# Batch 1's transposes by DMA, keys of batch 2 loaded sooner, and the first x in halves: an attention and FFN kernel on one core

## The chip, the cores and the metric

The kernel runs on one core of a Trainium2 chip. The metric is the device time of one execution in microseconds (us). Seven runs of the kernel before the change took 249.07 to 250.13 us, with a median of 249.35 us.

## The reference

Two stages follow each other. An attention without softmax (a "cosformer") is computed for 8 batches of 8 heads, 576 positions and head dimension 64; its output, as 4608 tokens of 512 values, goes through an FFN in which two projections are multiplied with each other.

```python
# q, k, v: [8, 8, 576, 64]; theta = pi/2 * pos / 576
def phi(x, c, s):
    r = np.maximum(x, 0.0)
    return np.concatenate([r * c, r * s], axis=-1)      # 64 -> 128 features
q_p, k_p = phi(q, cos_w, sin_w), phi(k, cos_w, sin_w)
kv = np.einsum('bhsf,bhsd->bhfd', k_p, v)
z = np.sum(k_p, axis=2)
num = np.einsum('bhsf,bhfd->bhsd', q_p, kv)
den = np.einsum('bhsf,bhf->bhs', q_p, z)[..., None] + 1e-06
x = (num / den).transpose(0, 2, 1, 3).reshape(4608, 512)
# FFN: w1, w2 [512, 1024], w3 [1024, 1024], w_out [1024, 512]
out = ((x @ w1) * (x @ w2)) @ w3 @ w_out
```

## The kernel before

**Attention.** Each batch is cut into five chunks: four of 128 positions and one (chunk 4) of 64. Even batches take them in the order 0, 1, 2, 3, 4, odd batches in the order 4, 0, 1, 2, 3. The inputs are loaded by the POOL queue (`load`, lines 133 and 137, each tensor in a part 0 of 320 KB and a part 1 of 256 KB for the inner batches). `features` (lines 265 to 272) makes the cosine half of the features on DVE and the sine half on ACT. `kv_chunk` multiplies keys with values and sums up over the chunks in the PSUM tile `pnum`; column 64 of each head's values is one, so z comes along. The sum is copied to `kvs`.

The queries must stand with their features on the partitions. There are two ways to that. `q_tr` transposes a chunk's 8 heads on TensorE (PE) and copies the result from PSUM to `qpT`. In the other, `prep_q` issues one DMA transpose from the SP queue (line 283). `dma_q(b)` lists the chunks of a batch that go the second way: none of batch 0, chunks 1, 2 and 3 of batch 1, and all from batch 2 on.

`num(b, c)` multiplies `qpT` with `kvs` for the 8 heads (line 355) into `pnum`, of which there is one buffer, and `normalize` divides on DVE (lines 363 to 365: add, reciprocal, multiply), giving `xblk`, 512 values per token. Chunk 0 of batch 0 has a PSUM tile of its own, `pfirst`.

`x_tr(b, c)` transposes `xblk` into `xT`, which holds 512 tokens per FFN tile. In batches 0 and 1 it uses four PE transposes (line 392) and a copy from PSUM on ACT or DVE (line 394); from batch 2 on it is one DMA transpose on the SP queue (line 387). The tokens of batch 1 fill the rest of FFN tile 1 and the start of tile 2.

**FFN.** There are nine tiles (t) of 512 tokens. For each, `ffn_groups` gives matmuls with w1b and w2b (line 464), a copy `asb` on ACT and the product `abT` on DVE, and then matmuls with w34b (line 510). w34b is w3 times w_out, made in the kernel while tile 0 is worked on (`w3_tr`, line 220, and `w34_mm`, line 232). Tile 0 starts in quarters of 128 tokens, so that PE has work as soon as the first x is there.

**Order.** The schedule is manual: each engine's instructions run in the order in which the program writes them. `ffn_groups` is a generator; after each of its steps the work listed in `slots[g]` is written. For tile 0 the list is made by hand. In slot 15 stands a second list, `between`, spread over the 16 steps of `w34_mm`, whose entries 16 to 23 go to the later slots and 24 to 31 to tile 1. `attention_at(1, between, kv, tr, nu, xt)` places batch 1's steps by the position in the order 4, 0, 1, 2, 3: `tr` where a chunk is transposed on PE, `nu` where `num` stands, and `xt` where `x_tr` stands. From batch 2 on `plan_batch` does this with a fixed pattern.

Loads on the POOL queue are held back by tiny copies: `behind_k`, `behind_q` and `behind_x` copy one element of a result to `seen` (line 540), so that POOL waits for it, and then issue the load. `other_loads` is such a sequence, released by the first `xblk`: the remaining weights, w3 in eight parts, and k, q and v of batch 1. The DMA transposes of SP and the loads of POOL use the same 16 DMA engines.

Of the kernel before, what the change touches and what calls it, by code (L numbers as in the profile page):

```python
# [13 lines left out]
ALU = mybir.AluOpType  # L14
# [3 lines left out]
H, S, D = 8, 576, 64  # L18
# [50 lines left out]
def kernel(  # L69
# [11 lines left out]
    nc = tc.nc  # L81
# [28 lines left out]
    def load_first(eng, t, src, c0=0, n=4, b=0, rows=slice(0, P)):  # L110
        at = src[b, :, 0:512, :].rearrange("h (p j) d -> p h j d", j=4)
        eng.dma_start(out=t[rows, :, c0:c0 + n, :].rearrange("p h j d -> p h (j d)"),  # L112
                      in_=at[rows, :, c0:c0 + n, :].rearrange("p h j d -> p h (j d)"))

    def load_first4(eng, t, src, b=0):
        eng.dma_start(out=t[0:64, :, 4, :], in_=src[b, :, 512:S, :].rearrange("h p d -> p h d"))

    def raw_tile(name):
        return ld.tile([P, H, NCH, D], BF16, name=name + "s", bufs=2 if name == "k" else 1)

    def load(b, which, part=None):
        for name in which:
            src = {"k": k, "v": v, "q": q}[name]
            if part != 1:
                raw[b, name] = raw_tile(name)
            if b in own:
                half = slice(64 * part, 64 * part + 64)
                load_first(nc.gpsimd, raw[b, name], src, b=b, rows=half)
                if part == 1:
                    load_first4(nc.gpsimd, raw[b, name], src, b=b)  # L130
                continue
            if part != 1:
                nc.gpsimd.dma_start(
                    out=raw[b, name][0:64, :, :, :].rearrange("p h j d -> p h (j d)"),
                    in_=src[b, :, 0:320, :].rearrange("h (p j) d -> p h (j d)", j=5))
            if part != 0:
                nc.gpsimd.dma_start(
                    out=raw[b, name][64:128, :, 0:4, :].rearrange("p h j d -> p h (j d)"),
                    in_=src[b, :, 320:S, :].rearrange("h (p j) d -> p h (j d)", j=4))
# [9 lines left out]
    def load_w3(jp):  # L149
        nc.gpsimd.dma_start(out=w3b[:, jp, :], in_=moe_w3[ts(jp, P), :])  # L150
# [36 lines left out]
    identb = const.tile([P, P], BF16, name="identb")  # L187
# [4 lines left out]
    def load_w12(c0, n):  # L192
        nc.gpsimd.dma_start(out=w1b[:, :, ds(c0, n)], in_=w1v[:, :, ds(c0, n)])
        nc.gpsimd.dma_start(out=w2b[:, :, ds(c0, n)], in_=w2v[:, :, ds(c0, n)])
# [6 lines left out]
    def other_loads(behind):  # L201

        seen = sm.tile([P, 1], BF16, name="seen", bufs=1)
        nc.gpsimd.tensor_copy(out=seen[:], in_=behind)
        nc.gpsimd.dma_start(out=w2b[:, :, ds(512, 256)], in_=w2v[:, :, ds(512, 256)])
        load_w12(768, 256)
        nc.gpsimd.dma_start(out=woutb[:], in_=moe_w_out.rearrange("(c p) m -> p c m", p=P))
        for jp in range(8):
            load_w3(jp)
            if jp == 4:  # L210
                load(1, "k")
        load(1, "qv")


    w3Ts = {}
# [22 lines left out]
    def order_of(b):  # L238

        return [0, 1, 2, 3, 4] if b % 2 == 0 else [4, 0, 1, 2, 3]  # L240

    def dma_q(b):

        return order_of(b)[5 if b == 0 else 2 if b == 1 else 0:]

    feat = {}

# [5 lines left out]
    att = {}  # L253
# [91 lines left out]
    def num(b, c, chain=True):  # L345
        rows = out_rows(b, c)
        R = ROWS[c]
        at = columns_of(b, c) - rows.start
        qpT, kvs = att[b]["qpT"], att[b]["kvs"]
        if b == 0 and c == 0:  # L350
            nt = ps_first.tile([P, 2, 512], FP32, name="pfirst")
        else:
            nt = ps_att.tile([P, 2, 512], FP32, name="pnum")
        for h in range(H):
            nc.tensor.matmul(nt[:, h // 4, ds((h % 4) * 65, 65)], lhsT=qpT[:, h, ds(at, 128)],  # L355
                             rhs=kvs[:, h, :], start=True, stop=True)
        n4 = nt[rows, :, 0:260].rearrange("p g (h e) -> p g h e", e=65)
        xblk = sm.tile([P, 2, 4, D], BF16, name="xblk", bufs=6)
        att[b]["x"][c] = xblk

        def normalize():
            den = sm.tile([P, 2, 4], FP32, name="den")
            nc.vector.tensor_scalar_add(out=den[rows], in0=n4[:, :, :, 64], scalar1=1e-6)  # L363
            nc.vector.reciprocal(out=den[rows], in_=den[rows])
            nc.vector.tensor_tensor(out=xblk[rows], in0=n4[:, :, :, 0:D],  # L365
                                    in1=den[rows].unsqueeze(3).to_broadcast([R, 2, 4, D]),
                                    op=ALU.mult)

        if chain:
            normalize()  # L370
        return normalize

    xT = {}

    def x_tr(b, c, by_vector=False, pst=None):
        R, rows = ROWS[c], out_rows(b, c)
        xblk = att[b]["x"].pop(c)
        xf = xblk[rows].rearrange("p g h d -> p (g h d)")
        if b % 2 == 0:
            slot = S * b + 128 * c  # L380
        else:
            slot = S * b + (0 if c == 4 else 64 + 128 * c)
        t, o = divmod(slot, 512)
        if t not in xT:
            xT[t] = xtp.tile([P, 4, 512], BF16, name="xT")
        if b >= 2:
            nc.sync.dma_start_transpose(out=xT[t][:, :, ds(o, R)], in_=xf)
            return
        if pst is None:
            pst = ps_tr.tile([P, 8, 128], BF16, name="pst")  # L390
        for kc in range(4):
            nc.tensor.transpose(pst[:, kc, 0:R], xf[:, ts(kc, 128)], identb[rows, rows])  # L392
        copy = nc.vector.tensor_copy if by_vector else nc.scalar.copy
        copy(out=xT[t][:, :, ds(o, R)], in_=pst[:, 0:4, 0:R])  # L394

    def attention_at(b, slots, kv, tr, nu, xt):

# [151 lines left out]
    def behind_q(b, i, *what):  # L549
        behind(feat[b][1][0:64, order_of(b)[i], 0, 0:1], *what)  # L550
# [37 lines left out]
    for c in range(NCH):  # L588
# [19 lines left out]
         pst=unread[:, :].bitcast(BF16).rearrange("p (a b) -> p a b", b=128))  # L608
# [13 lines left out]
    for t in range(NT):  # L622
        slots = [[] for _ in range(24)]
        if t == 0:
            slots[1].append(lambda: x_tr(0, 1, by_vector=True))
            slots[1].append(lambda: q_tr(0, 3, evac=False)[1]())
            slots[1].append(lambda: num(0, 2))
            slots[3].append(lambda: num(0, 3))
            slots[3].append(lambda: x_tr(0, 2))
            slots[5].append(lambda: x_tr(0, 3))  # L630
            slots[6].append(lambda: prep_q(0, 4))
            slots[11].append(lambda: feature_buffers(1))
            slots[8].append(lambda: q_tr(0, 4))
            slots[10].append(lambda: num(0, 4))
            slots[12].append(lambda: x_tr(0, 4))
            slots[14].append(lambda: w3_tr(0))
            between = [[] for _ in range(32)]
            spread(prep_units(1, (prep_k,)), 6, 8, between)
            spread(prep_units(1, (prep_q,)), 10, 12, between)
            spread(prep_units(1, (prep_v,)), 13, 13, between)  # L640
            attention_at(1, between, kv=(14, 14, 14, 14, 14), tr=(12, 13, 17, 18, 19),
                         nu=(15, 17, 19, 20, 25), xt=(20, 20, 21, 22, 27))
            later = between[24:32]
            for i in range(2):
                between[11 + i].append(lambda i=i: behind_q(1, 2 + 2 * i, 2, "k", i))
            for i, g in enumerate((15, 17, 17, 19)):
                between[g].append(lambda i=i: behind_x(1, (i + 1) // 2, 2, "vvqq"[i], i % 2))
            for jp in range(8):
                for part in range(2):
                    if part == 0 and jp < 7:  # L650
                        slots[15].append(lambda jp=jp: w3_tr(jp + 1))
                    slots[15].append(lambda jp=jp, part=part: w34_mm(jp, part))
                    slots[15] += between[2 * jp + part]
            for g in range(16, 24):
                slots[g] += between[g]
            slots[16].append(open_held)
        elif t == 1:
            for g, units in enumerate(later):
                slots[g] += units
        for g in range(24):  # L660
            slots[g] += plan[24 * t + g]
        for g, _ in enumerate(ffn_groups(t)):
            for u in slots[g]:
                u()
# [30 lines left out]
```

## Time and profile before

| | before |
|---|---|
| median of 7 runs | 249.35 us |
| the profiled execution | 249.5 us |
| its span from first to last instruction | 247.7 us |
| PE busy | 241.5 us |
| VectorE (DVE) busy | 142.7 us |
| ScalarE (ACT) busy | 123.1 us |
| GpSimd (POOL) busy | 94.0 us |
| granted TensorE clock | full |
| HBM traffic over the span | 195 GB/s |

The profile comes from one execution; its own time is 0.15 us above the median of the runs. Times in it count from the first instruction. "The chain of waits" is the work that ended last, followed back step by step to what released it. PE is TensorE's matmul stream and PEld its loading of weights, which overlaps with it; a matmul's end is modelled, so neighbouring matmuls overlap in the timeline, and what PE needs for one is read from the distance between starts or from the chain. A bracket behind an instruction of the timeline tells how long its engine stood idle before it, and on whose result. For a DMA the time to landing runs from its issue to its semaphore.

### The profile page before, as it was taken

The numbers are of one execution on the slowest core, as the hardware profiler recorded it, in microseconds if no ns is written. First come the engines' busy times: TensorE is split into PE (matmuls) and PEld (weight loads), VectorE is DVE, ScalarE is ACT, GpSimd is POOL, SyncE is SP. The second block draws the span as 40 slices with busy tenths as digits, with TensorE's granted clock in tenths as the row PEclk, the third lists the DMA queues.
The fourth block names the chain that finished last, engine by engine and source line by source line (L and its number), as shares of the span: only waits on it lengthen the run. The fifth ranks groups of instructions, "written<-read, shape, count | busy, mean of one in ns | idle before, by whom it ended". The sixth has DMA issues, their size and how long they took to land.

```text
span 247.7 us, 4927 instructions
## 1 busy us (share of the span) xinstructions
PE 241.5 (98%) x1839; PEld 127.4 (51%) x1839; DVE 142.7 (58%) x333; ACT 123.1 (50%) x209; POOL 94.0 (38%) x189
## 2 busy tenths in 40 slices
PE   8899999999999999999999999999999999999994
PEld 2478555565454545544544555455545554444443
DVE  7776674756658555748465866576586555312421
ACT  2576324927762594268426832773287332323331
POOL 7655142215512442154113621562153007875400
PEclk9999999999999999999999999999999999999999
DMA  6999999999999999999999899999985927998713
GB/s 192 177 194 198 210 204 205 145 154 190 167 128 203 148 138 137 150 153 168 138 128 151 110 157 150 154 179 137 149 112 148 210 57 170 285 294 271 211 40 131
DMA packets 86087, 41.15 MB, mean 166 GB/s; under 512 B 53552, under 2 KB 82608, under 8 KB 86064
## 3 DMA queue, kind: packets, MB, share of 16 engines
q0 software_dynamic: 37072, 27.20, 74.0%
q1 hardware_dynamic: 48560, 13.18, 33.1%
q10 hardware_dynamic: 432, 0.46, 0.5%
q8 instruction: 14, 0.23, 0.3%
q14 instruction: 9, 0.07, 0.1%
HBM read 38.80 MB, written 9.44 MB: 195 GB/s over the span
## 4 chain that ended last, share of the span: by engine, by line
PE 93%; DMA 3%; DVE 1%; issue 1%; POOL 1%; ACT 0%; POOLq 0%
PE ffnps L464 50%; PE ffnps L510 24%; PE ffnps L232 6%; PE pnum L355 4%; PE pnum L297 4%; DMA qs<-in_q_dram 3%; PE pst L220 1%; PE pst L392 1%; PE pst L328 1%; PE ffnps L527 1%; POOL vs L112 0%; DVE xblk L365 0%; PE pfirst L355 0%; ACT xT L394 0%; DVE qpT L342 0%
## 5 line engine op out<-in xcount | busy, mean ns | idle before, releaser
L505 DVE TENSOR_TENSOR abT<-asb,ffnps 128x512 bf16<-128x512 bf16 x68 | 46.6, 686 | 55.1 <-PE ffnps L464 54.3
L464 PE MATMUL ffnps<-xT,w1b 128*128 128x512 bf16 (+2 forms) x320 | 74.9, 357 | 0.4 <-ACT xT L394 0.2
L464 PE MATMUL ffnps<-xT,w2b 128*128 128x512 bf16 (+2 forms) x320 | 74.9, 357 | 0.0
L510 PE MATMUL ffnps<-w34b,abT 128*128 128x512 bf16 x280 | 65.8, 379 | 0.0
L501 ACT CAST asb<-ffnps 128x512 bf16<-128x512 f32 x68 | 39.8, 585 | 48.6 <-PE ffnps L464 47.2
L516 ACT COPY held<-ffnps 128x512 f32<-128x512 f32 x35 | 20.5, 586 | 49.6 <-PE ffnps L510 47.6
L464 PEld LDWEIGHTS <-w1b 128*128 128x128 bf16 x320 | 28.9, 98 | 27.7 <-issue 0.6
L464 PEld LDWEIGHTS <-w2b 128*128 128x128 bf16 x320 | 28.7, 98 | 26.9
L510 PEld LDWEIGHTS <-abT 128*128 128x128 bf16 x280 | 25.6, 98 | 26.4
L269 ACT ACTIVATE qp<-qs,sinv 128x512 bf16<-128x512 bf16 (+2 forms) x40 | 28.3, 716 | 3.2 <-DMA qs<-in_q_dram 3.2
L365 DVE TENSOR_TENSOR xblk<-pnum,den 128x512 bf16<-128x512 f32 (+1 forms) x39 | 27.0, 691 | 2.2
L438 POOL DMA_DIRECT2D out_dram<-held x42 | 22.2, 534 | 6.4 <-DMA out_dram<-held 3.7
L269 ACT ACTIVATE kp<-ks,sinv 128x512 bf16<-128x512 bf16 (+1 forms) x35 | 24.5, 721 | 0.0
L540 POOL COPY seen<-xblk 64x1 bf16<-64x1 bf16 x15 | 2.8, 184 | 53.3 <-DVE xblk L365 53.3
L355 PEld LDWEIGHTS <-qpT 128*128 128x128 bf16 x320 | 15.0, 98 | 10.2 <-issue 2.7
L265 DVE TENSOR_SCALAR qp<-qs,cosv 128x512 bf16<-128x512 bf16 (+1 forms) x40 | 17.4, 439 | 2.0 <-DMA qs<-in_q_dram 2.0
L540 POOL COPY seen<-qp 64x1 bf16<-64x1 bf16 x14 | 2.6, 184 | 40.4 <-DVE qp L265 40.4
L363 DVE TENSOR_SCALAR den<-pnum 128x8 f32<-128x8 f32 (+1 forms) x39 | 6.4, 165 | 19.4 <-PE pnum L355 19.4
L289 POOL COPY va<-vs 128x512 bf16<-128x512 bf16 (+1 forms) x30 | 17.5, 632 | 0.0
L297 PEld LDWEIGHTS <-kp 128*128 128x128 bf16 x280 | 13.0, 98 | 7.3
L355 PE MATMUL pnum<-kvs,qpT 128*128 128x65 bf16 x312 | 16.4, 194 | 0.0
L232 PE MATMUL ffnps<-woutb,w3T 128*128 128x512 bf16 x64 | 15.4, 379 | 0.0
(87 smaller groups left out, 184.5 us busy)
## 6 DMA issues: line engine op xcount, KB each, us to landing
out_dram<-held POOLq DMA_DIRECT2D x16, 256.0 KB, 5.1
out_dram<-held POOLq DMA_DIRECT2D x24, 128.0 KB, 4.1
qs<-in_q_dram POOLq DMA_DIRECT2D x10, 256.0 KB, 5.9
w3b<-in_moe_w_dram POOLq DMA_DIRECT2D x8, 256.0 KB, 13.1
ks<-in_k_dram POOLq DMA_DIRECT2D x8, 256.0 KB, 6.5
vs<-in_v_dram POOLq DMA_DIRECT2D x8, 256.0 KB, 6.7
ks<-in_k_dram POOLq DMA_DIRECT2D x6, 320.0 KB, 6.0
qs<-in_q_dram POOLq DMA_DIRECT2D x6, 320.0 KB, 5.7
```

The source lines that it names most:

```text
L232: nc.tensor.matmul(acc[:, :], lhsT=w3T[:, lc, :], rhs=woutb[:, lc, :], start=(lc == 0), stop=(lc == 7))
L269: nc.scalar.activation(out=dst[:R, c, 0:n, D:F], in_=src[:R, 0:n, c, :], func=ACTF.Relu, scale=sinv[:R, at:at + 1], bias=0.0)
L289: eng.tensor_copy(out=feat_of(b)[2][:R, c, :, 0:D], in_=raw[b, "v"][:R, :, c, :])
L297: nc.tensor.matmul(kvt[:, h // 4, ds((h % 4) * 65, 65)], lhsT=kp[:, c, h, :], rhs=va[:, c, h, 0:D + 1], start=(i == 0 and h % 4 == 0), sto ...
L355: nc.tensor.matmul(nt[:, h // 4, ds((h % 4) * 65, 65)], lhsT=qpT[:, h, ds(at, 128)], rhs=kvs[:, h, :], start=True, stop=True)
L365: nc.vector.tensor_tensor(out=xblk[rows], in0=n4[:, :, :, 0:D], in1=den[rows].unsqueeze(3).to_broadcast([R, 2, 4, D]), op=ALU.mult)
L438: eng.dma_start(out=rows[:, :, cols], in_=osb[64 * i:64 * i + rows.shape[0], :, cols])
L464: nc.tensor.matmul(out, lhsT=w[:, kc, ts(jc, 128)], rhs=x[:, kc, tok], start=(kc == 0), stop=(kc == 3))
L501: nc.scalar.copy(out=asb[:], in_=aT[:, :])
L505: nc.vector.tensor_mul(out=abT[:, jc, :], in0=asb[:], in1=bT[:, :])
L510: nc.tensor.matmul(ops[:, :], lhsT=abT[:, jc, ts(ms, 128)], rhs=w34b[:, jc, :], start=(jc == 0), stop=(jc == 7))
L516: nc.scalar.copy(out=osb[:, ms % 2, :], in_=ops[:, :])
```

## The change

It has four parts.

- Batch 1: chunk 0 of the queries joins chunks 1 to 3 on the DMA path (`dma_q`). `x_tr` of chunks 3 and 4 becomes a DMA transpose on SP. Their places in the order (`xt`) go from 20 to 15 for chunk 4 and from 27 to 25 for chunk 3, right behind their `num`. `x_tr` keeps the reference to `xblk`, because `behind_x` reads it afterwards.
- Keys of batch 2: part 0 is loaded at the end of `other_loads` instead of behind the query features of chunk 1 of batch 1, part 1 behind those of chunk 4 instead of chunk 3. (The position in the order, not the chunk number, is what `behind_q` takes: before, positions 2 and 4; after, position 0.)
- The first x (batch 0, chunk 0): the multiply of `normalize` runs in two halves of four heads, and `x_tr` transposes two blocks and copies them, then the other two, both on DVE.
- Chunk 3 of batch 0: `x_tr` likewise runs in two halves; the first is copied by ACT, the second by DVE.

```diff
@@ other_loads
         load(1, "qv")
+        load(2, "k", 0)
@@ dma_q
-        return order_of(b)[5 if b == 0 else 2 if b == 1 else 0:]
+        return order_of(b)[5 if b == 0 else 1 if b == 1 else 0:]
@@ num, normalize
-            nc.vector.tensor_tensor(out=xblk[rows], in0=n4[:, :, :, 0:D],
-                                    in1=den[rows].unsqueeze(3).to_broadcast([R, 2, 4, D]),
-                                    op=ALU.mult)
+            n = 1 if b == 0 and c == 0 else 2
+            for i in range(2 // n):
+                g = ts(i, n)
+                nc.vector.tensor_tensor(out=xblk[rows, g], in0=n4[:, g, :, 0:D],
+                                        in1=den[rows, g].unsqueeze(3).to_broadcast([R, n, 4, D]),
+                                        op=ALU.mult)
@@ x_tr
-        xblk = att[b]["x"].pop(c)
+        xblk = att[b]["x"][c]
...
-        if b >= 2:
+        if b >= 2 or b == 1 and c >= 3:
             nc.sync.dma_start_transpose(out=xT[t][:, :, ds(o, R)], in_=xf)
             return
...
-        for kc in range(4):
-            nc.tensor.transpose(pst[:, kc, 0:R], xf[:, ts(kc, 128)], identb[rows, rows])
-        copy = nc.vector.tensor_copy if by_vector else nc.scalar.copy
-        copy(out=xT[t][:, :, ds(o, R)], in_=pst[:, 0:4, 0:R])
+        copies = [nc.vector.tensor_copy if by_vector else nc.scalar.copy] * 2
+        if b == 0 and c == 3:
+            copies[1] = nc.vector.tensor_copy
+        n = 2 if b == 0 and c in (0, 3) else 4
+        for i in range(4 // n):
+            for kc in range(n * i, n * i + n):
+                nc.tensor.transpose(pst[:, kc, 0:R], xf[:, ts(kc, 128)], identb[rows, rows])
+            copies[i](out=xT[t][:, ts(i, n), ds(o, R)], in_=pst[:, ts(i, n), 0:R])
@@ the slots of tile 0
-                         nu=(15, 17, 19, 20, 25), xt=(20, 20, 21, 22, 27))
+                         nu=(15, 17, 19, 20, 25), xt=(15, 20, 21, 22, 25))
...
-            for i in range(2):
-                between[11 + i].append(lambda i=i: behind_q(1, 2 + 2 * i, 2, "k", i))
+            between[10].append(lambda: behind_q(1, 0, 2, "k", 1))
```

## The prediction

> **What bounds the kernel now.** I began with the page's busy shares and the shares of the chain that ended last, to find the engine that sets the end.
>
> ```profile
> PE 241.5 (98%) x1839; PEld 127.4 (51%) x1839; DVE 142.7 (58%) x333; ACT 123.1 (50%) x209; POOL 94.0 (38%) x189
> ...
> PE 93%; DMA 3%; DVE 1%; issue 1%; POOL 1%; ACT 0%; POOLq 0%
> ```
>
> A busy PE need not be a full PE, so the second line matters more: 93% of the chain is matmuls and the DMA part is the first load of queries. Next the chain in order of time (start, length, what), at the places that the change touches:
>
> ```profile
> 21.88 0.24 PE pst L392 x4
> ...
> 22.14 0.59 ACT xT L394
> ...
> 22.77 3.66 PE ffnps L464 x36
> ...
> 49.62 0.45 PE pst L328 x8
> ...
> 58.24 0.55 PE pst L392 x8
> ...
> 65.86 0.30 PE pst L392 x4
> ```
>
> After 22.77 the chain is PE piece after PE piece. So every transpose there costs its own length, and one taken off PE gives that back, until something else is late. The timeline shows what is nearly late (start, length, engine, line; idle time before it in brackets):
>
> ```profile
> 17.20 0.23 PEld L392 LDWEIGHTS <-xblk 128*128 128x128 bf16 x4 [0.19 <-DVE xblk L365]
> ...
> 22.77 0.38 PE L464 MATMUL ffnps<-xT,w1b 128*128 128x128 bf16 x4 [0.23 <-ACT xT L394]
> ...
> 46.61 0.72 ACT L269 ACTIVATE qp<-qs,sinv 128x512 bf16<-128x512 bf16 x1 [0.41 <-DMA qs<-in_q_dram]
> ...
> 57.85 0.69 DVE L365 TENSOR_TENSOR xblk<-pnum,den 128x512 bf16<-128x512 f32 x1
> ...
> 58.66 0.32 PEld L355 LDWEIGHTS <-qpT 128*128 128x128 bf16 x8
> ```
>
> Last, the tile qpT, for its first DMA transpose (issue length in ns, issue time, time to landing):
>
> ```profile
> L283 SPq DMA_TRANSPOSE qpT<-qp x1: 1332/1332/1332, 48.5 to 48.5; - x1
> ...
> DMA to landing us min/median/max: 8.0/8.0/8.0
> ```
>
> It was issued at 48.46 and landed at 56.4; its user, num(1,1), ran at 56.95. That is half a microsecond of room, and decides the rivals.
>
> **What the Trainium skill says.** "TensorE: Matmul & The Clock Gate", section "Back-to-back issue gap": an isolated warm matmul costs N/2.4 + 2.5 ns, 56 ns at 128 columns. The chain's 0.22 us for four (the piece at 61.06) and 0.45 for eight agree. "VectorE: DVE Perf Modes", section "The three transpose paths", lists the crossbar DMA as slower for one 128x128 block (1309 ns against 390 ns on TensorE). Here one instruction does eight blocks, SP needs about 1.25 us to issue it, and landing takes 2.7 to 9.3 us: latency, not PE time. "DMA: Bandwidth & Descriptors", section "Issuing engines are not separate DMA queues": transfers of SP and POOL run on the same 16 engines and interleave. The trace agrees: between 77 and 79 us the POOL queue moved 490 packets and SP's 534.
>
> **The change part by part.**
>
> *q_tr(1,0) goes to DMA.* Off PE: 8 transposes, 0.45 us by the chain (49.62). What follows is w34_mm and kv_chunk(1). The latter starts 0.45 earlier, about 50.3, and needs the first va chunk, ready by 49.6; its last chunk comes 1 us later than its start, its va being ready at 50.5. So no new wait: **-0.45**. The DVE copy of 0.68 us that goes was beside PE work. Added: one SP issue at about 47.4, since the ACT feature behind the DMA landing at 46.59 ends at 47.33; chunks 1 to 3 queue behind it on SP by up to 1.3 us. num(1,0) needs the landing by 54.97 - 0.65 = 54.3, so it has 6.9 us.
>
> *x_tr(1,4) goes to DMA.* The two x_tr of that slot take from 58.07 (L510's end) to 58.69, 0.62 us; one full x_tr takes 0.22. So 0.40 could go. But num(1,2) follows, and it needs the one pnum buffer, which the DVE multiply frees at 58.54 (57.85 + 0.69). With the usual 0.06 to the PE, num(1,2) can start at 58.60 instead of 58.69: **-0.09**, the remaining 0.3 becoming a wait on DVE. The copy on ACT (0.37) was hidden. The DMA is issued near 54.0, or once SP's queue is through; FFN tile 1 needs it at 61.98 - 0.74 = 61.2.
>
> *x_tr(1,3) goes to DMA.* PE loses the piece at 65.86, its wait included: **-0.29**. Its tile is used only by FFN tile 2, past 85 us. It passes ahead of qpT of batch 2 on SP; their first issue is at 67.30 and this one's source is ready at 65.7, so it is through (1.2 us) in time. An ACT copy of 0.57 goes, hidden.
>
> *x_tr(0,3) in halves, on ACT and DVE.* Now: four transposes from 21.71, ACT copy 22.14 to 22.73, FFN at 22.77, where PE could have gone on at 22.38. After: the first pair is ready 0.11 earlier, its ACT copy takes 0.37 (row 128x256, 374 ns), 22.03 to 22.40. The DVE copy of the other pair waits for the abT multiply (21.70 + 0.69 = 22.39) and takes 0.30 by the rows for 512 and 1024 elements (425 and 678 ns): to 22.65. Blocks 0 and 1 of FFN start at 22.44, block 2 at 22.69 instead of 22.88: **-0.2** (bounds 0 and 0.39, the whole wait).
>
> *First x normalized and copied in halves.* The multiply of 691 ns becomes two of 424 by the page's (N+151)/0.96 ("VectorE: DVE Perf Modes", the TRN2 errata, which gives 691 for 512 as traced). The copy of 425 becomes two of about 298. The DVE feature instruction that sits between them ends at 15.5, the copies end near 15.95 instead of 16.07, and FFN starts at 15.8 to 16.0 instead of 16.13. But after 16 matmuls PE already waits 0.19 for xblk of chunk 1 (the line at 17.20). That comes from num(0,1), released at 15.49 by the ACT copy of qpT, which nothing here moves. So the 0.2 to 0.3 becomes a longer wait: **0**. Bounds: +0.1 if two more DVE instructions push den(0,1) back, -0.1 for a shorter chain.
>
> *Keys of batch 2.* The first half moves from behind_q (issue at 47.81) into other_loads behind v of batch 1. POOL issues at 38.78 and waits for an earlier landing each time, so about 40.1, with POOL idle until 47.36 in any case. It lands behind v (about 49.4 plus 1.6 for 320 KB at 200 GB/s). The second half is issued near 46.8 instead of 49.17. POOL issues the same number of DMAs. The copies that gate v and q of batch 2 keep their order, with PE's shift. The copy that releases other_loads reads only the first half of the first x, so it may run 0.27 earlier (14.95), in front of a queue of loads that is full anyway. Worth nothing by itself; the move clears 50 to 55 us for the transposes: **0**, if the cover holds.
>
> Sum: -0.45 - 0.09 - 0.29 - 0.2 = **-1.0 us**. After 65 us the chain stays PE, with POOL's gates moving along, so it reaches the end. The profiled execution took 249.5 (span 247.7 and 1.8 around it): it becomes 248.5. The median, 249.35, lies 0.15 lower: **248.35**.
>
> **Rivals.**
>
> *The transposes land late (slower).* Chunk 0 is issued at 47.4, while v and both halves of k are still in the POOL queue: 0.58 MB from about 47.5. If packets alternate, SP's queue gets a third of the bytes, some 60 KB/us, and 256 KB take 4.3 us, starting only when the stream allows; before, the first packets of this queue appeared 3.4 us after the issue. 51 + 4.3 + 1 gives a landing near 56.3. num(1,0) then stalls 2 us, in order on PE with everything behind it, and the result is 250.4. For it: the 8.0 us row. Against: in batch 2 the same first transpose landed 3.3 us after its issue, and the loads that lay among the transposes (49.2 to 57.2) now end near 51. The point of decision: a landing of chunk 0 after 54.3 eats into the gain, after 55.3 there is none, after 55.8 it is slower by over 0.2%. xT(1,4) after 62.2 would do the same.
>
> *Part of the gain is lost.* With the 8.0 us latency unchanged chunk 0 lands at 55.4, PE waits 1.1 us, and the time is 249.4: no change. Half of that wait gives 248.9.
>
> *More than summed.* If the pnum wait is shorter than read and the whole of x_tr(1,4) counts (0.3 more), and x_tr(0,3) gets 0.39: 247.9.
>
> *The moved transposes were hidden anyway.* That would need slack on PE behind them; the only PE waits over 0.1 us after 22.77 are a few of 0.16 from 76 us on. Then 249.2.
>
> **How the numbers follow.** Forecast -0.7 to -1.3: 0.60. More than summed: 0.06. Part lost 0.17, of which 0.05 is still faster by over 0.2% (0.5 us, about what a measurement of this kernel can tell from no change). Hidden anyway: 0.03. Slower: 0.14. Faster 0.71, same 0.15, slower 0.14. The range goes from 247.7 (more than summed, with the 0.1 that the first x could bring) to 249.9, which takes in the lost gain and the start of the late landing.
>
> **What would show it.** Right: the transposes of q_tr number 40 instead of 48 and those of x_tr 32 instead of 40; no PE wait on a DMA at num(1,0) near 54.3; num(1,2) waiting about 0.3 us for xblk; the wait at 17.20 grown to about 0.45; FFN after x_tr(0,3) near 22.5. Wrong: a wait of num on the DMA of qpT, or of L464 on xT, between 54 and 63 us; or later q features in batch 2 (66.55 now), which would show the DMA queues as the new limit.

## The result, and the profile after

| | before | after |
|---|---|---|
| median | 249.36 us (30 runs) | 250.95 us (12 runs) |
| lowest to highest | 249.0 to 251.8 | 250.1 to 252.1 |
| the profiled execution | 249.5 | 250.78 |
| its span | 247.7 | 249.0 |

The ratio is 1.0061 with a 95% interval of 1.0044 to 1.0077: slower by 0.6%, or 1.5 us. The forecast was 248.35 us, so sign and size are both wrong, and 250.95 lies outside the range. A run more than 1.5% above the fastest of its kernel counts as slow and is left out of every ratio; that is one run in all, of 253.82 us, in d2 below.

The page first, its busy shares and the shares of the chain that ended last:

```profile
PE 240.0 (96%) x1823; PEld 126.5 (51%) x1823; DVE 141.4 (57%) x335; ACT 122.0 (49%) x207; POOL 94.1 (38%) x188
...
PE 85%; DMA 9%; DVE 1%; ACT 1%; issue 1%; POOL 1%; POOLq 0%
```

PE has 16 matmuls fewer, the eight of q_tr and the eight of the two x_tr, and is busy for 1.5 us less; the span is 1.3 us longer. The chain's PE share fell from 93% to 85% and its DMA share rose from 3% to 9%: the work was taken off PE, and PE now waits for what replaced it. The list of PE's waits (engine, line, what it waited for; us in total, times, longest) names the places; those ahead of num(0,0) are left out:

```profile
...
PE pnum L356 <- DMA qpT<-qp: 0.9, 2, 0.7
PE unread L401 <- DVE xT L402: 0.5, 1, 0.5
PE pst L401 <- ACT xT L402: 0.5, 1, 0.5
PE pnum L356 <- DVE xblk L369: 0.2, 1, 0.2
...
PE ffnps L472 <- ACT kp L270: 0.2, 1, 0.2
```

Of these only a wait of num for xblk had been forecast. The next table compares the start of the same instruction in both traces (us), so that each step of the difference gets a place. The row of num(0,0) is the difference with which the two executions began. `asb` is the ACT copy out of an FFN group: it follows PE closely.

| instruction | before | after | difference | what happened since the row above |
|---|---|---|---|---|
| num(0,0) | 13.36 | 13.14 | -0.22 | the first queries landed earlier; the change doesn't touch this |
| asb, first of tile 0 | 19.06 | 19.13 | +0.07 | +0.29: first x in halves |
| asb, third of tile 0 | 23.64 | 23.99 | +0.35 | +0.28: x_tr(0,3) in halves |
| num(1,4) | 52.99 | 53.64 | +0.65 | -0.45: q_tr(1,0) off PE; +0.74: new wait for the DMA of qpT |
| num(1,2) | 58.69 | 59.35 | +0.66 | x_tr(1,4) off PE brought nothing |
| FFN behind num(1,3) | 66.00 | 66.36 | +0.36 | -0.30: x_tr(1,3) off PE |
| num(2,1) | 76.32 | 76.95 | +0.63 | +0.27: wait for the DMA of qpT |
| an asb of tile 3 | 110.55 | 111.51 | +0.96 | +0.32: FFN tile 3 waits, as it seems for the DMA of xT |

Counted from num(0,0) that is 1.18 us, since this execution began 0.22 earlier. From there to the last matmul the difference stays at 0.96. The other 0.35 of the 1.3 lies behind the last matmul, where SP waits for the landing of the last stores. From the list of SP's waits, before and after:

```profile
SPq L690 <- DMA out_dram<-held: 1.2, 2, 0.9
```

```profile
SPq L697 <- DMA out_dram<-held: 1.8, 2, 1.6
```

The stores themselves land no later: the last one 2.33 us behind the start of the last matmul before, 2.38 after. What changed is the order in which SP asks for them. In the traces the DMAs of SP and ACT use eight semaphores in turn, and the closing waits stand in a fixed order, each taking at least 0.06 us. Before, the last stores signal to semaphores near the end of that order. With the three DMA transposes more of the change they have moved round to its beginning, so that the other waits are still to come when the last store has landed. From the start of the last matmul to the end of the span it is 3.32 us before and 3.67 after. The traces of the experiments below agree without exception: 3.23 to 3.33 us in the six kernels with at most one SP DMA more than the kernel before (68 or 69), and 3.65 to 3.70 in the eleven with two or three more (70 or 71).

**The halves.** This is the chain of waits of the kernel after, from 15 to 23 us (start, length, what):

```profile
15.27 0.21 DVE xT L402
15.48 0.04 issue
15.52 0.28 PE unread L401 x2
15.80 0.02 issue
15.83 0.30 DVE xT L402
16.13 0.04 issue
16.17 1.05 PE ffnps L472 x16
...
21.94 0.13 PE pst L401 x2
22.07 0.02 issue
22.09 0.38 ACT xT L402
22.47 0.04 issue
22.52 0.27 PE pst L401 x2
```

Both pieces have one shape: two transposes, a copy, and only then the other two transposes. The second pair starts 0.04 us after the copy of the first pair ends. The forecast let it follow the first pair directly. In the order of PE eight FFN matmuls stand behind the second pair that in the kernel before filled this time. In the timeline the same instruction carries the length of that wait (idle time before it in brackets):

```profile
22.52 0.27 PE L401 MATMUL pst<-identb,xblk 128*128 128x128 bf16 x2 [0.46 <-ACT xT L402]
```

Both pairs write one PSUM tile, and the copy reads that tile. The Trainium skill, "PSUM — Partial Sum Buffer", section "PSUM bank collisions raise a hardware error", says that a write by TensorE and a read by another engine must be kept apart by bank and quarter of the partitions, not by address. That the four blocks don't overlap is therefore no help. The waits of 0.46 and 0.50 agree with such an order, and the runs with two tiles below show what takes them away. In these the second half changes its tile and its bank together, so whether the order goes by tile or by bank is not shown.

**The wait of num(1,4).** Before, num(1,4) ran without a bracket, that is, with no wait on a result:

```profile
52.99 0.42 PE L355 MATMUL pnum<-kvs,qpT 128*128 128x65 bf16 x8
```

The chain of the kernel after from 47 to 60 us:

```profile
47.28 6.31 DMA qpT<-qp
53.59 0.05 issue
53.64 0.43 PE pnum L356 x8
...
58.52 0.70 DVE xblk L369
59.22 0.14 issue
59.35 0.42 PE pnum L356 x8
```

The tile qpT in the window of the first DMA transpose, which is now that of chunk 0 (issue length in ns, issue time, who waited, time to landing):

```profile
L284 SPq DMA_TRANSPOSE qpT<-qp x1: 1332/1332/1332, 47.3 to 47.3; - x1
...
  PEld L356: 1.2, 1
  PE pnum L356: 0.7, 1
...
DMA to landing us min/median/max: 6.3/6.3/6.3
```

Before, this tile's first transpose needed 8.0 us to land; now 6.3. The issue time was forecast within 0.1 us (47.4). But the num that waits is num(1,4), not num(1,0). Chunk 4 of an odd batch holds 64 positions in columns 0 to 63, and `num` reads `qpT[:, h, ds(at, 128)]` from `at` = 0: 128 columns, of which 64 to 127 belong to chunk 0. Their 64 output rows are never used, but the load of weights waits for their landing. num(1,4) stands two slots, 2 us, ahead of num(1,0).

**Later waits.** From 69 to 110 us the chain holds two more pieces that are no work of PE:

```profile
69.72 7.18 DMA qpT<-qp
76.90 0.05 issue
76.95 0.43 PE pnum L356 x8
...
109.09 1.34 ACT kp L270 x2
110.45 7.07 PE ffnps L472 x32
```

num(2,1) waits for its queries. Their transpose was issued at 69.72 and took 7.18 us; before, it was issued at 68.88 and took 3.1, landing 4.3 us ahead of its use. The later issue comes from the queries, which landed 1.1 us later than before (67.55 against 66.47), their load having been issued 0.67 later. The longer flight goes mostly with the x of chunk 3, which went out ahead on the SP queue (66.39, landed 72.69). In all ten traces with xT(1,3) on the DMA this transpose took 5.5 to 7.6 us. Of the seven without, five show 3.1 to 3.3, but d4 and e1 show 5.3 and 6.5, so it isn't that alone. The second piece is put down to ACT's kp, which doesn't feed an FFN matmul. What fits is the DMA of the last part of tile 3's x, xT(3,1): issued 104.99, landed 110.36 (before: 104.34 and 108.22). The first matmul of tile 3 starts 0.09 us after that landing here, and also in a4 and c1; no run isolates it.

### The profile page after: what moved, and what is told of

Its sections match the earlier page's. It is cut to its first block, busy times and chain, and to the rows that moved or that the text cites. A ratio compares the mean times of both kernels' runs of the same rounds, so it can differ in the third digit from the quotient of the medians.

```text
span 249.0 us, 4903 instructions
## 1 busy us (share of the span) xinstructions
PE 240.0 (96%) x1823; PEld 126.5 (51%) x1823; DVE 141.4 (57%) x335; ACT 122.0 (49%) x207; POOL 94.1 (38%) x188
## 4 chain that ended last, share of the span: by engine, by line
PE 85%; DMA 9%; DVE 1%; ACT 1%; issue 1%; POOL 1%; POOLq 0%
PE ffnps L472 47%; PE ffnps L518 23%; DMA qpT<-qp 5%; PE pnum L356 4%; PE ffnps L233 4%; DMA qs<-in_q_dram 3%; PE pnum L298 3%; PE pst L221 1%; PE ffnps L535 1%; PE pst L401 1%; DVE xblk L369 1%; ACT kp L270 1%; ACT qp L270 0%; POOL vs L112 0%; PE pst L329 0%
## 5 line engine op out<-in xcount | busy, mean ns | idle before, releaser
L266 DVE TENSOR_SCALAR qp<-qs,cosv 128x512 bf16<-128x512 bf16 (+1 forms) x40 | 16.8, 426 | 2.9 <-DMA qs<-in_q_dram 2.9
```

## The experiments

The edits are named once here and then combined. "Whole", "narrow", "two tiles" and "late" start from the kernel after:

```diff
# whole: both x in one piece again
-            n = 1 if b == 0 and c == 0 else 2
+            n = 2
-        n = 2 if b == 0 and c in (0, 3) else 4
+        n = 4
# narrow: num(1,4) loads its own 64 columns
+        w = 64 if b == 1 and c == 4 else 128
-            nc.tensor.matmul(nt[:, h // 4, ...], lhsT=qpT[:, h, ds(at, 128)],
+            nc.tensor.matmul(nt[0:w, h // 4, ...], lhsT=qpT[:, h, ds(at, w)],
# two tiles: the second half of a halved x in another PSUM tile
         for i in range(4 // n):
+            if i == 1:
+                pst = second if second is not None else ps_tr.tile([P, 8, 128], BF16, name="pst")
# late: keys of batch 2 as in the kernel before
-        load(2, "k", 0)
-            between[10].append(lambda: behind_q(1, 0, 2, "k", 1))
+            for i in range(2):
+                between[11 + i].append(lambda i=i: behind_q(1, 2 + 2 * i, 2, "k", i))
```

For the first x, `second` is the bank of `kva`, which is free by then. All ratios are to the kernel before on the same chip, with 95% intervals. The a runs were on one chip, b, c and d on a second, e on a third. Where the text says how far PE is ahead, this is counted from num(0,0) unless it says otherwise, because the executions begin with differences of up to 0.55 us that no edit made.

| run | edit | median us | ratio |
|---|---|---|---|
| a1_whole_x | after, whole | 250.49 | 1.0049 (1.0035 to 1.0063) |
| a2_halves_alone | before, with the halves alone | 250.24 | 1.0029 (1.0016 to 1.0042) |
| a3_narrow | after, narrow | 250.35 | 1.0024 (1.0010 to 1.0038) |
| a4_whole_narrow | after, whole and narrow | 249.63 | 0.9995 (0.9980 to 1.0011) |
| b5_whole_narrow_late | a4, late | 252.70 | 1.0135 (1.0119 to 1.0151) |
| b2_whole_narrow_x13pe | a4, x_tr(1,3) on PE | 249.65 | 1.0008 (0.9997 to 1.0018) |
| b3_whole_narrow_x14pe | a4, x_tr(1,4) on PE | 249.33 | 1.0000 (0.9987 to 1.0013) |
| c1_two_tiles_narrow | after, two tiles and narrow | 249.16 | 0.9994 (0.9985 to 1.0002) |
| d1_two_tiles_narrow_x14pe | c1, x_tr(1,4) on PE | 249.19 | 0.9984 (0.9972 to 0.9996) |
| d2_d1_q4_later | d1, a load of queries moved | 249.27 | 1.0002 (0.9984 to 1.0020) |
| d3_two_tiles_alone | before, with halves in two tiles | 249.20 | 0.9990 (0.9970 to 1.0010) |
| d4_q10_narrow_keys | before, chunk 0 by DMA, narrow, early keys | 249.00 | 0.9979 (0.9967 to 0.9991) |
| e1_d4_two_tiles | d4, with halves in two tiles | 248.78 | 0.9985 (0.9975 to 0.9994) |
| e2_x_dma_alone | before, x_tr(1,3) and (1,4) by DMA | 249.55 | 1.0023 (1.0010 to 1.0037) |
| e3_keys_alone | before, early keys | 249.24 | 0.9999 (0.9983 to 1.0015) |

### The two suspects: a1, a2, a3, a4

The theory from these traces: the halves cost 0.57 us, and num(1,4) waits 0.74 for columns that it doesn't use. The rival: the DMA queues as a whole are overloaded, and the wait appears elsewhere if one is removed.

> The changed kernel with both x in one piece again (normalize of the first x whole; x_tr of chunks 0 and 3 of batch 0 with four transposes and one copy); all else as changed. Theory, the halves wait on each other: in the changed kernel's trace the second pair of transposes waits for the copy of the first pair out of the same PSUM tile (0.50 us on DVE, 0.46 on ACT), which put PE 0.29 and 0.28 us back by 24 us. Expected: about 0.57 us faster than the changed kernel, so 1.0 us above the kernel before (ratio 1.004), with num(1,4) still waiting for the DMA transpose. Rival, the halves are hidden and the whole loss lies in the DMA transposes: no difference to the changed kernel, ratio 1.006.

Measured: 1.0049. Without the halves PE reaches num(1,4) earlier, at 52.02 instead of 52.81, and the transpose lands only 0.3 sooner: the whole idle time there grows from 0.83 to 1.30, and num(1,4) starts at 53.32 instead of 53.64. In this trace most of what the halves cost is hidden behind the other fault. The interval takes in both the ratio expected and that of the rival, so the median alone decides nothing.

> The kernel before with the halves alone (normalize of the first x, x_tr of chunks 0 and 3 of batch 0). Theory, the halves wait on each other: 0.57 us slower than before, 249.9 us, ratio 1.0023, and the chain stays PE after 24 us. Rival, my prediction's step: 0.2 us faster, ratio 0.999.

Measured: 1.0029, or 0.7 us slower. Its PE is 0.29 later at 19 us, 0.57 at 24 us and 0.64 at the end. So the halves lose time by themselves, where -0.2 had been forecast.

> The changed kernel, but num(1,4) loads only its own 64 columns of qpT as weights, not 128, of which the upper 64 are chunk 0's. Theory, the wait is num(1,4)'s needless read of chunk 0: it starts again right after kvs, at about 52.9 us, num(1,0) is not needed before 54.9, after the landing at 53.6; 0.74 us faster than changed, about 250.2 us, ratio 1.003. Rival, the DMA queues are the new limit: the wait only moves to num(1,0) or num(1,1), ratio 1.005 to 1.006.

Measured: 1.0024. The timeline of this kernel at num(1,4), weights and matmuls:

```profile
52.87 0.33 PEld L357 LDWEIGHTS <-qpT 128*64 128x64 bf16 x8 [0.42 <-issue]
52.87 0.44 PE L357 MATMUL pnum<-kvs,qpT 128*64 128x65 bf16 x8
```

The wait for the DMA is gone, although chunk 0 landed at 53.28, after num(1,4) had begun. Only the width of the read was changed, so the unused columns were the cause. PE is 0.26 behind before at the first asb of tile 1 (65 us) and level with it at the end of the profiled run, which took 249.57. The median of 22 runs is 0.8 higher than that run, and what the slower ones wait for was not caught.

> Both edits: x in one piece and num(1,4) with 64 columns. If both theories hold the gains add to 1.3 us: 249.6 us, ratio 1.001; what is left over the kernel before would be the waits of batch 2 and later (0.28 us at num(2,1), 0.3 us at FFN tile 4) against 0.75 us of PE work taken off. If the DMA queues are the limit: ratio 1.004.

Measured: 0.9995, no change to before. In its profile PE is 0.61 us ahead of before as far as 107 us. There most of it is lost in one wait:

```profile
109.32 1.02 PE L473 MATMUL ffnps<-xT,w1b 128*128 128x512 bf16 x4 [0.49 <-ACT kp L270]
```

This is FFN tile 3 again, from start to start 0.66 us late, and again the profile puts it down to kp. xT(3,1) was issued at 103.52, 0.8 earlier than before, and landed at 109.23, 1.0 later than before: 5.7 us where before took 3.9. PE arrives earlier and the transpose arrives later. At the last matmul PE is 0.08 behind before, and the closing waits add 0.33. Both theories hold in part: taking out the two faults takes away the loss of 1.5 us, and in this profile a DMA transpose that lands late and the closing waits keep the gain.

### The cover of the early keys: b5, e3

> Whole x and 64 columns, and the keys of batch 2 loaded late again, as in the kernel before (behind positions 2 and 4 of the query features). If the early load clears the way for the transposes, chunk 0 lands later than 53.4 us: 8 us after its issue at 46.8, about 54.8 us, and num(1,0) near 54.2 us waits 0.6 us or more, with chunks 1 and 2 behind it; ratio 1.002 to 1.004. Rival, the keys only change places in the queue: landing as before, ratio 0.9995.

Measured: 1.0135, 3.4 us slower than before (4 runs). The timeline at num(1,1), and the tile qpT in the window of chunk 1's transpose:

```profile
58.37 0.43 PE L356 MATMUL pnum<-kvs,qpT 128*128 128x65 bf16 x8 [2.12 <-DMA qpT<-qp]
```

```profile
L283 SPq DMA_TRANSPOSE qpT<-qp x1: 1610/1610/1610, 48.1 to 48.1; - x1
...
DMA to landing us min/median/max: 10.2/10.2/10.2
```

With the two halves of the keys among the transposes, chunk 1 takes 10.2 us, and num(1,1) stalls 2.12. Chunk 0 landed at 53.44, as in a4 and not at 54.8 as expected: the queue fails one chunk later and costs far more. It is the effect that the prediction's slower rival feared, transposes behind the bytes of POOL, but the rival expected it with early keys, and it comes with late ones.

This profile loses 1.5 us more behind the stall. From 59.4 to 62.8 us the granted clock of TensorE was 0.5 instead of 1.0. The other three runs show a mean clock of 0.999 to 1.0 and were as slow, so the loss of the median doesn't rest on it.

> The kernel before with the keys of batch 2 loaded early and nothing else. The prediction's step: nothing by itself, ratio 1.000, with the three query transposes of batch 1 landing about 3 us earlier than at 56.4, 57.9 and 58.8 us. Rival, the early load is in something's way: above 1.001.

Measured: 0.9999. The three transposes of batch 1 land at 53.49, 55.83 and 56.56 instead of 56.4, 57.9 and 58.8, and no time comes of it, since their users were not waiting. Worth nothing alone and 1.4% as cover (0.9995 against 1.0135, on two chips): the same edit.

### The x of batch 1 on the DMA: b3, b2, e2

> Whole x and 64 columns, but x_tr(1,4) on PE again in slot 20. By the prediction's step PE loses nothing or 0.1 us, because num(1,2) waits for the multiply that frees pnum anyway (the wait of 0.39 us before num(1,2) falls to 0.07): ratio 0.9995 to 1.000. Rival, the whole 0.4 us of the two transposes counts: ratio 1.001.

Its edit, in a4:

```diff
-        if b >= 2 or b == 1 and c >= 3:
+        if b >= 2 or b == 1 and c == 3:
-                         nu=(15, 17, 19, 20, 25), xt=(15, 20, 21, 22, 25))
+                         nu=(15, 17, 19, 20, 25), xt=(20, 20, 21, 22, 25))
```

Measured: 1.0000. The wait for xblk before num(1,2) is gone, and across this stretch PE keeps its difference to before in both kernels (0.32 ahead with x_tr(1,4) on PE, 0.31 with it on the DMA). Four transposes less on PE were worth 0.00 us: num(1,2) can't start until the multiply has freed `pnum`, and it starts 0.145 us after the end of that multiply in the kernel before as in those after. This profile has no wait at FFN tile 3: PE is 0.62 ahead to the last matmul, and xT(3,1) took 3.9 us. The wait in a4 is therefore no fixed price of these edits.

> Whole x and 64 columns, but x_tr(1,3) on PE again in slot 27. The PE work comes back: 0.30 us slower than with the DMA (1.0007), unless the DMA ahead of the queries of batch 2 on SP costs as much: then the transposes of batch 2 are issued and land earlier than at 70.9 and 75.2 us, num(2,1) has more room and the time is the same (0.9995).

The same edit for chunk 3 (`c == 4` stays on the DMA, last `xt` 27). Measured: 1.0008. Its profiled run, 249.05 and the fastest of its 21, began 0.49 us early and keeps 0.30 more to the last matmul; the median is 0.6 above it. The transposes of batch 2 did land earlier, at 69.8 and 71.0 us. Against a4 no difference can be told.

> The kernel before with x_tr(1,3) and x_tr(1,4) by DMA in their new places and nothing else. The prediction's steps: -0.09 and -0.29, ratio 0.9985. Theory now: the two transposes stand in SP's queue ahead of those of batch 2 and beside POOL's loads, and the lead is given back (and more) where PE waits for a landing, at num(1,1) to num(1,2) or at the first matmul of FFN tiles 1 to 3: ratio 1.000 to 1.003, with a wider spread of the runs.

The diff of `x_tr` and `xt` alone, on the kernel before. Measured: 1.0023, slower. Its profile, of a run of 249.3, shows PE 0.30 ahead from x_tr(1,3) to the last matmul, and no new wait but 0.2 for xblk. The closing waits take that back: they are 0.35 us longer with the two SP DMAs more. So this run has nothing left of the gain, but it doesn't show the loss either. 8 of the 22 runs took over 250 us, against 3 of the 51 of the kernel before. What those 8 wait for was not caught in a profile. The wait at 76.95 in the kernel after is a candidate: in e2's profile the same transpose took 6.7 us and landed 0.26 us ahead of num(2,1), where the kernel before has 4.3 us. It is not shown for this kernel.

### Halves that work: c1, d3

> The changed kernel with the 64 columns for num(1,4), and with the second half of each halved x in a second PSUM tile (kva's bank for the first x, another pst for chunk 3). Theory, the halves lose because the second pair of transposes waits for the copy of the first pair out of the same tile: with two tiles the wait in the middle goes, and PE stands by 24 us where the prediction had it: 0.2 us ahead of the kernel with whole x, 0 for the first x. So 0.5 to 0.7 us faster than the kernel with halves and 64 columns (1.0024), ratio about 0.998 to 0.999. Rival, more and smaller instructions are the cost: as with one tile, PE 0.3 us back by 24 us, ratio 1.002.

Measured: 0.9994. The timeline at x_tr(0,3), with DVE and ACT:

```profile
21.66 0.39 PE L404 MATMUL pst<-identb,xblk 128*128 128x128 bf16 x4
...
21.97 0.37 ACT L405 COPY xT<-pst 128x256 bf16<-128x256 bf16 x1 [0.36 <-PE pst L404]
...
22.25 0.28 DVE L405 COPY xT<-pst 128x256 bf16<-128x256 bf16 x1
...
22.40 0.47 PE L475 MATMUL ffnps<-xT,w1b 128*128 128x128 bf16 x4
```

All four transposes run in one go, the copies overlap, and the FFN matmuls that need this x start 0.74 us behind the first transpose instead of 1.06 in the kernel before (21.71 to 22.77). Measured at the asb behind it this is -0.20 us for x_tr(0,3) and -0.04 for the first x: close to the two numbers of the prediction (-0.2 and 0), which were right for this form of the edit and not for the one that the change has. FFN tile 3 takes most of the gain back here too: it waits 0.67 at 109.25.

> The kernel before with the halves in two PSUM tiles each and nothing else. The prediction's step for the halves, without the wait in the middle: 0.2 us faster than before (0.9992), PE 0.2 us ahead from 24 us on to the end; with one tile each the same edit had ratio 1.0029. Rival, the halves cost by their number: above 1.001.

Measured: 0.9990, with an interval that reaches 1.001. The profile shows PE 0.25 ahead at 24 us and 0.14 at the end. The interval can't separate so little from nothing, but it lies wholly below that of a2 (1.0016 to 1.0042), the same edit with one tile each.

### Where the gain goes: d1, d2

> Two PSUM tiles for each halved x, 64 columns for num(1,4), chunk 0 of the queries and x_tr(1,3) by DMA, x_tr(1,4) on PE. By the offsets of the traces so far: -0.2 (chunk 3 of batch 0) -0.45 (q_tr) -0.3 (x_tr(1,3)) to the end of batch 1, and up to 0.7 given back where FFN tile 3 waits for the DMA transpose of x(3,1): between 248.4 and 249.1 us, ratio 0.996 to 0.999.

Measured: 0.9984. Its profiled run took 250.44, against a median of 249.19, and so shows what can happen in single runs. PE is 0.87 ahead until FFN tile 2:

```profile
86.79 1.02 PE L475 MATMUL ffnps<-xT,w1b 128*128 128x512 bf16 x4 [1.08 <-DMA xT<-xblk]
```

xT(2,1) was issued at 78.00 and landed at 86.35, after 8.35 us. The queue of POOL issued 320 KB of queries at the same moment:

```profile
78.16 0.68 POOL L133 DMA_DIRECT2D qs<-in_q_dram  x1 [0.36 <-issue]
```

Transposes of xT in this run took 3.9 us in the median. The Trainium skill, "DMA: Bandwidth & Descriptors", section "Issuing engines are not separate DMA queues", fits this: both queues run on the same engines. The other traces bear it out. Where this load was issued from 0.1 us before to 0.2 us after xT(2,1) (after, a1, a4, d1), the transpose took 5.8 to 8.35 us; in the other 13 traces the load came 0.4 to 0.65 us after it, and it took 3.8 to 4.5. No run moved this load alone, so that the load is the cause is likely and not shown. From 87 us on this run is behind the kernel before.

> The same, with the first half of the queries of batch 4 loaded behind position 2 of x of batch 3 instead of position 1, so that it no longer runs beside the transpose of x(3,1) (issued at 103.5, landed at 109.2 with FFN tile 3 waiting 0.67 us for it in two of the traces). Theory, the lead is given back at tile 3 through the shared DMA engines: the transpose lands about 4 us after its issue, the wait at tile 3 goes, and the time is 0.3 to 0.7 us below the run without this edit. Rival, that wait is chance and not that load's doing: same time.

```diff
-            if b + 1 < B and i in (1, 3):
-                plan[z + 7 + 2 * i].append(lambda i=i: behind_x(b, i, b + 1, "q", i // 2))
+            at = (2, 3) if b == 3 else (1, 3)
+            if b + 1 < B and i in at:
+                plan[z + 7 + 2 * i].append(lambda i=i, n=at.index(i): behind_x(b, i, b + 1, "q", n))
```

Measured: 1.0002, with runs from 248.5 to 251.8 and 5 of 21 above 250. In its profile xT(3,1) still took 5.3 us, and PE loses 0.22 of its lead at tile 3. Moving one load by one chunk does not settle the matter, and whether that load is what delays xT(3,1) stays open. Over all traces xT(3,1) took 3.8 to 4.3 us in eight (before, a2, b3, d3, d4, e1, e2, e3) and 5.0 to 5.7 in the other nine, although the load was issued 1.4 to 1.5 us ahead of it in all but d2. Two of the eight, b3 and e2, have x of batch 1 on the DMA.

### What is worth keeping: d4, e1

> The kernel before with chunk 0 of batch 1's queries by DMA, 64 columns for num(1,4) and the early keys; x untouched. The prediction's first step alone: PE 0.45 us ahead from 50 us on, 248.9 us, ratio 0.998. Rival, the DMA engines give it back in later batches: PE ahead at 62 us but not at 120 us, ratio 1.000.

The lines of `dma_q` and of the keys from the change, and "narrow", on the kernel before; x_tr stays as it was. Measured: 0.9979, faster, and none of its 22 runs above 250 us. In the profile PE is 0.32 us ahead from the first asb of tile 1 to the end: 0.45 less 0.13 that PE loses within and behind the matmuls with 64-column weights.

> Chunk 0 of batch 1's queries by DMA with 64 columns for num(1,4) and early keys, both halved x in two PSUM tiles, and no x of batch 1 by DMA. PE steps: -0.3 (query chunk, less the 0.1 that the 64-column weights cost) and -0.2 (chunk 3 of batch 0). If they add: 248.8 to 248.9 us, ratio 0.9975 or a little lower, below the same kernel with x(1,3) by DMA (0.9984), which has 0.3 us less PE work. Rival, x(1,3) by DMA keeps its 0.3 us in the median: this one is slower than that, ratio 0.999.

Measured: 0.9985 and 248.78 us, the lowest median of all, against 249.16 for the kernel before on that chip. From its page:

```profile
span 246.6 us, 4885 instructions
...
PE 92%; DMA 3%; issue 1%; DVE 1%; POOL 1%; POOLq 0%
```

The chain is PE again, with the DMA share back at 3%. The intervals of d4 and e1 overlap: both beat the kernel before, by 0.5 and 0.4 us as the ratios have it, and neither is shown to be better than the other. The expected ratio of 0.9975 was missed, and e1 is level with d1 (0.9984), which has x(1,3) on the DMA as well. The traces say why that x brings nothing there: it takes 0.30 us off PE, and with it d1's closing waits are 0.46 us longer than e1's (3.69 against 3.23).

## Why the prediction was wrong

**q_tr(1,0), forecast -0.45.** The PE time was right: without its wait num(1,4) would have started 0.45 earlier relative to what stands ahead of it. The step that failed is "num(1,0) needs the landing by 54.97 - 0.65 = 54.3, so it has 6.9 us". The landing, 53.59, met that time. The first reader of chunk 0's columns is num(1,4), which needed it at 52.9. In the kernel before this overlap cost nothing, since chunk 0 was transposed on PE well ahead. Narrowing the read to 64 columns removed the wait (a3), and with that the part is worth 0.32 in the trace and, with the early keys, 0.2% in the median (d4). The slower rival had the right kind of wait, a num that waits for a DMA transpose, with the wrong place and deadline and for the wrong reason: the transposes were not late, chunk 0 landing 0.7 us ahead of the time that the forecast allowed.

**x_tr(0,3) in halves, forecast -0.2; first x, forecast 0.** The failed step is "the first pair is ready 0.11 earlier", with the second pair taken to follow at once. Waits of 0.46 and 0.50 for the copy out of the same PSUM tile make these parts +0.28 and +0.29. With two tiles they measured -0.20 and -0.04 (c1). The two halves of the multiply, which the prediction estimated at 424 ns each from the page's formula, took 424 and 415 ns; so the cost of the smaller instructions was rightly forecast. For the first x the forecast sign "wait at 17.20 grown to about 0.45" stayed away: it is 0.21 at 17.27, since the halves delayed PE itself:

```profile
17.27 0.23 PEld L401 LDWEIGHTS <-xblk 128*128 128x128 bf16 x4 [0.21 <-DVE xblk L369]
```

**x_tr(1,4), forecast -0.09.** Its limit was right: num(1,2) waits for xblk. The bracket shows 0.23; from start to start the stall is 0.39, 0.3 being forecast. What is left is nothing rather than 0.09 (b3). The step that failed is "the usual 0.06 to the PE". In the prediction's own lines the multiply ends at 58.54 and num(1,2) starts at 58.69, 0.145 later, and the kernels after show 0.146. num(1,2) was already waiting for the multiply before the change, and the two transposes were hidden.

**x_tr(1,3), forecast -0.29.** The trace gives -0.30. The step that failed is the cost of the DMA that replaces the transposes. The prediction put it at nothing with "so it is through (1.2 us) in time". That held for SP's issue: xT(1,3) went out at 66.39, and the first transpose of batch 2's queries, at 68.38, waited for its features. But xT(1,3) was in flight until 72.69, the transpose for num(2,1) took 7.2 us instead of 3.1, and num(2,1) gave 0.27 back. The features of batch 2's queries began at 67.63 instead of 66.55, the sign that the prediction had named for the DMA queues as a new limit; 0.67 us of that is the later issue of their load. With the longer close of the program (0.35) nothing of the 0.30 is left. As a median the two x of batch 1 on the DMA cost 0.2% (e2), and what carries the rest of that is open, as said.

**The end of the program, "so it reaches the end".** The forecast moved PE's gain to the end and let what follows the last matmul stay as it was. It became 0.35 us longer, because the order of SP's closing waits no longer fits the last stores.

**After 65 us, "the chain stays PE".** It does not. FFN tile 3 waits for xT(3,1) in the kernel after and, longer, in a4 and c1, which arrive there earlier. The prediction had no room for a wait of batch 3, because it took the landing times of before as fixed. They are not: the same transpose took 3.9, 5.4 and 5.7 us.

**Early keys, forecast 0 with the cover as their purpose.** Right on both counts (e3, b5).

Where the +1.5 us comes from is then: +0.57 halves, +0.74 num(1,4), +0.59 two later DMA waits, -0.75 off PE, and +0.35 at the end of the program. The profiled run's 0.22 of earlier start is not the change's.

## What to carry to other kernels

Before an operand is moved to a slower path, look up every instruction whose access touches its bytes, not only the one that needs the values: a read padded to full width takes the deadline of its padding. Splitting a transpose and its copy overlaps them only if the halves have PSUM tiles of their own. Where the gain of one stage makes PE arrive earlier at operands that come by a shared DMA queue, ask for the room at each of these arrivals, and judge by many runs, because one profile can show the gain and miss the runs that lose it. When the number of DMAs changes, look behind the last matmul too, where the program waits for its stores.

## What was not expected of the hardware

- A DMA transpose of the same size has no fixed latency. From issue to landing those of qpT for 128 positions took 3.1 to 8.6 us in the kernel after, and 10.2 in b5, and those of xT for 128 tokens 2.4 to 8.35 in d1.
- Weights of 64 columns beside those of 128 are not free: PE lost 0.09 us behind num(1,4) and 0.03 within it (a3). The gap of 0.31 in front of num(1,4) is the same with 128 columns, in the kernel before.
- The spread of the runs differs between kernels: above 250 us were 8 of 22 in e2 and 3 of 51 of the kernel before beside it, which is hardly chance. The 0 of 22 in d4 against 7 of 66 may be. The chip may count too: on that of the a runs the kernel before has 11 of 52.
- A long wait of PE can cost more than itself. Behind the 2.12 us in b5 the granted clock was 0.5 for 3.4 us; behind the 1.08 us in d1 it stayed at 1.0.
- The close of a program depends on how many DMAs were issued before it: 3.2 to 3.3 us or 3.65 to 3.7 behind the start of the last matmul, with the last store landing at 2.3 to 2.4 in every trace.
